# Four last chunks as two wide blocks, softmax steps ordered by a modelled clock, w_out sums on POOL

## The chip, the cores and the metric

The kernel runs on one core of a Trainium2 chip. The metric is the device time of one execution in microseconds (us). Engines are named as in the profile: PE is TensorE (matmuls, PEld its weight loads), DVE is VectorE, ACT is ScalarE, POOL is GpSimd, SP is SyncE, whose queue issues the DMAs.

## The reference, cut to what matters

Sliding-window attention of 8 batches x 8 heads over 576 positions of 64, then an MLP with elu on the 4608 tokens.

```python
scores = scale * np.matmul(q, k.transpose(0, 1, 3, 2))      # (8, 8, 576, 576), scale 1/8
mask_plain = (rel >= 0) & (rel < 32)                        # heads 0-3
mask_dil = (rel >= 0) & (rel < 128) & (rel % 4 == 0)        # heads 4-7
scores = np.where(masks, scores, -1e9)
attn = np.exp(scores - np.max(scores, -1)); attn = attn / (np.sum(attn, -1) + 1e-09)
x = (attn @ v).transpose(0, 2, 1, 3).reshape(4608, 512)
h = x @ w_in                                                # 512 x 2048
g = np.where(h > 0, h, np.exp(np.minimum(h, 0)) - 1)        # elu
out = g @ w_out                                             # 2048 x 512
```

## The kernel before

Every float32 operand of the MLP is split into a high part and a low rest, and a product is three products of parts. The 4608 tokens are nine chunks of 512. Chunks 0 to 2 multiply plainly. From chunk 3 (`CS`) on, the products are of the Strassen kind: seven products of half-sized operands take the place of eight, and sums and differences of blocks are made beside them on ACT and DVE.

- **Combined chunks** (3 to 6, `combined_chunk`): only h = x w_in is done with seven products. There are four groups `g` of seven steps, `ORDER` = A11 S2 S3 A12 S1 A22 S4; a step is 12 matmuls of 128x256 in `product`. A11, S2, S3 and A22 add up in one PSUM bank (`x_ps`), A12 in another (`y_ps`), which S1 opens anew and S4 adds to. Between them ACT copies the bank out: u1 after A11, u2 after S2, u3 after S3 (`TODO`, tile `e`), and DVE adds these to the other bank (C11 after A12, C22 after S1, C12 after S4). S2 and S3 write the bank that u1 and u2 read, so each waits for the copy. The second product of a group (elu(h) by w_out, 192 matmuls of 128x512 a chunk) waits in `fifo`; `pop(n)` after each step issues n parts of 3 matmuls, by `POPS`.
- **Wide block** (chunks 7 and 8 together, `wide_chunks`): both products are done with seven for eight, over 1024 tokens: 28 inner and 28 outer steps of 12 matmuls of 128x512. It needs sums of w_out blocks, made by `combine_out` on DVE and ACT (8 sets, each 4 sums of 128x256 and 2 rests of 128x512) in chunk 6 and in the block.
- **Attention** of batches 4 to 7 runs in the combined chunks. Heads go in pairs (four a batch). `PIECES` puts two pairs at a time between steps: a scores piece (144 matmuls, `scores_piece`) or an outputs piece (48 matmuls, `outputs_piece`). The softmax steps between them (`later_probabilities`: max, minus, exp on ACT, sum, reciprocal, times, then six small transposes a pair, all else on DVE) are put into the program by `work(SPARE[g][s])`, a budget for each step from a table.

Instructions of one engine keep program order (`inorder`). Helpers record many operations under one line: L124 is every matmul, L573 every ordered DVE and ACT instruction, L849 the load of stored w_in and w_out blocks (`load_combined`, four steps ahead by `RING`), L401 and L404 the copies of attention outputs.

Of the kernel before, what the change touches and what calls it, by code (L numbers as in the profile page):

```python
# [33 lines left out]
LASTC = NCH - 2  # L34
# [25 lines left out]
EARLY = 0.0  # L60
# [5 lines left out]
PIECES = {9: ("S", 2, 1), 14: ("O", 0, 1), 21: ("O", 2, 1), 23: ("S", 0, 2)}  # L66
# [20 lines left out]
def body(ctx: ExitStack, tc: tile.TileContext, q, k, v, masks, w_in, w_out, out, out_t):  # L87
# [35 lines left out]
    def mm(*args, **kw):  # L123
        return inorder(nc.tensor.matmul(*args, **kw))  # L124
# [204 lines left out]
    def combine_out(j):  # L329
# [3 lines left out]
        vec.tensor_tensor(out=a22, in0=a21, in1=a22, op=ALU.add)  # L333
        vec.tensor_tensor(out=a21, in0=a11, in1=a21, op=ALU.subtract)
        vec.tensor_tensor(out=a11, in0=a22, in1=a11, op=ALU.subtract)
        vec.tensor_tensor(out=a12, in0=a12, in1=a11, op=ALU.subtract)
        parts = []
        for w, names in zip(ws, (("S2", "S3"), ("S4", "S1"))):
            h, l = ap.tile([P, DM], F32R, name="vt"), w.bitcast(F32R)
            act.copy(out=h, in_=w)  # L340
            vec.tensor_tensor(out=l, in0=w, in1=h.bitcast(F32), op=ALU.subtract)
            parts += [(0, names, h), (1, names, l)]
        return parts
# [52 lines left out]
    def copies(b, hp, places, keep=lambda ins: ins):  # L396

        for a_ps, n0, n1 in places:
            flat, q0, q1 = a_ps[:, :(n1 - n0) * QB], n0 * QB, n1 * QB
            if hp >= NPAIR // 2:  # L400
                last = keep(nc.scalar.copy(out=x32[b][:, hp, q0:q1], in_=flat))  # L401
            else:
                dst = x32[b][:, hp, :].rearrange("p (c u) -> p c u", c=DIL)[:, :, q0 // DIL:q1 // DIL]
                last = keep(nc.scalar.copy(out=dst.rearrange("p c (s i) -> p s c i", i=G // DIL),  # L404
                                           in_=flat.rearrange("p (s c i) -> p s c i", c=DIL, i=G // DIL)))
        return last

# [159 lines left out]
    class Ordered:  # L567

        def __init__(self, eng):
            self.eng = eng  # L570

        def __getattr__(self, name):
            return lambda *args, **kw: inorder(getattr(self.eng, name)(*args, **kw))  # L573

    vec, act = Ordered(nc.vector), Ordered(nc.scalar)
    side, held = [], []

    def work(spare):

        while side and spare > 0:  # L580
            cost, step = side.pop(0)
            step()
            spare -= cost

    def later_probabilities(b, hps, groups):

        other_sm = slots("a5", 2, 3).rearrange("p o t -> p (o t)")[:QB, :2 * NU * 2 * G].rearrange("p (u j) -> p u j", u=2 * NU)
        sms = [ap.tile([QB, 2 * NU, 2 * G], F32, name="sm", bufs=1), other_sm]
        for j in (1, 0):
            masks_added(hps[j], groups[j], sms[j], vec)  # L590
        small = [[ap.tile([QB, 2 * NU], F32, name=n, bufs=4) for n in ("nmx", "sums")] for _ in hps]
        trs = [transposed() for _ in hps]
# [902 lines left out]
```

## Time and profile before

| | |
|---|---|
| median of 3 runs | 854.08 us (853.76 to 854.14) |
| profiled execution | 853.85 us, of which the profile's span is 852.0 us (1.85 us lie outside it) |
| mean granted TensorE clock | 0.997 of 2.4 GHz |
| PE busy | 839.9 us, 99% of the span |
| DVE, ACT, POOL busy | 657.6 us (77%), 486.5 us (57%), 8.7 us (1%) |
| chunk 3 begins at about | 317.5 us of the span |
| wide block | about 699.5 to 848.3 us |

Busy time is how long an engine had an instruction in it. The chain is followed back from the last instruction to what released it, so its shares say what the end of the kernel waited for.

### The profile page before, as it was taken

The page shows a single profiled execution, that of the slowest core. Times are in us where ns is not written, and L with a number is a line of the kernel's source. Part 1 is how long each engine was busy: PE and PEld are TensorE (multiplying, and loading weights), DVE is VectorE, ACT ScalarE, POOL GpSimd, SP SyncE. Part 2 cuts the span into 40 slices and gives each one's busy share as a digit, 9 for nine tenths or more (in the row PEclk, how much of TensorE's full clock was granted, in tenths as well). Part 3 has the DMA queues.
Part 4 walks back from the last instruction along what each step waited for, and adds up shares of the span by engine and source line. Part 5 has one row for each costly group of instructions (what it writes and reads, how often), then busy time and mean ns, then how long its engine had stood idle before and what let it go on. Part 6 is the DMA issues. An engine that isn't in the chain of part 4 may idle for free.

```text
span 852.0 us, 17515 instructions
## 1 busy us (share of the span) xinstructions
PE 839.9 (99%) x7080; PEld 704.0 (83%) x7080; DVE 657.6 (77%) x993; ACT 486.5 (57%) x835; POOL 8.7 (1%) x29
## 2 busy tenths in 40 slices
PE   6999999999999999999999999999999999999998
PEld 4566888888888889898999899899989988888886
DVE  5999998778588978965877587757877765786992
ACT  5889776645655465434644464544544556786460
POOL 3000000000000000000000000000000000000000
PEclk9999999999999999999999999999999999999999
DMA  8997457533677878757586667767675667997675
GB/s 301 378 378 304 138 170 237 163 112 107 204 253 237 266 206 258 242 181 244 179 262 195 193 219 221 251 186 218 193 237 189 212 209 240 334 353 247 188 222 170
DMA packets 99728, 193.73 MB, mean 227 GB/s; under 512 B 8800, under 2 KB 52160, under 8 KB 99648
## 3 DMA queue, kind: packets, MB, share of 16 engines
q1 hardware_dynamic: 99504, 192.30, 69.5%
q8 instruction: 56, 0.92, 0.4%
q10 hardware_dynamic: 144, 0.31, 0.1%
q14 instruction: 24, 0.20, 0.1%
HBM read 145.39 MB, written 47.19 MB: 226 GB/s over the span
## 4 chain that ended last, share of the span: by engine, by line
PE 97%; DMA 1%; ACT 1%; DVE 1%; issue 0%; SPq 0%; DVEq 0%; POOL 0%; ACTq 0%
PE o_ps L124 44%; PE h L124 41%; PE a_ps L124 11%; DMA r<-w_in 1%; DMA qt<-q 0%; ACT pt L490 0%; DVE nmx L450 0%; PE a L124 0%; DVE pt L488 0%; PE b L124 0%; PE d L124 0%; DVE sums L469 0%; ACT r L467 0%; DVE gh L573 0%; ACT x L404 0%
## 5 line engine op out<-in xcount | busy, mean ns | idle before, releaser
L124 PE MATMUL h<-xh,r 128*128 128x256 f32 (+1 forms) x728 | 171.7, 315 | 0.0
L124 PEld LDWEIGHTS h<-xh,r 128*128 128x128 f32 x728 | 123.6, 190 | 10.5 <-issue 0.2
L124 PE MATMUL o_ps<-a,r 128*128 128x512 f32 x528 | 127.0, 391 | 0.0
L124 PEld LDWEIGHTS o_ps<-a,r 128*128 128x128 f32 x528 | 97.3, 188 | 19.2
L124 PE MATMUL h<-xl,r 128*128 128x256 f32 (+1 forms) x364 | 109.0, 315 | 0.0
L124 PE MATMUL h<-a,r 128*128 128x256 f32 (+1 forms) x492 | 77.7, 308 | 0.0
L124 PE MATMUL o_ps<-a,gh 128*128 128x512 f32 x216 | 75.0, 444 | 0.0
L124 PEld LDWEIGHTS h<-a,r 128*128 128x128 f32 x492 | 69.6, 190 | 6.6
L124 PEld LDWEIGHTS h<-xl,r 128*128 128x128 f32 x364 | 69.3, 190 | 5.7 <-issue 0.2
L573 DVE SCALAR_TENSOR_TENSOR a-1_3460<-a-1_3460,a 128x1024 f32<-128x1024 f32 x32 | 39.1, 1222 | 37.3 <-ACT a L573 37.2
L573 ACT COPY e<-h 128x512 f32<-128x512 f32 x48 | 28.2, 588 | 56.3 <-PE h L124 55.5
L124 PE MATMUL o_ps<-r,r 128*128 128x512 f32 x220 | 57.5, 390 | 0.0
L124 PEld LDWEIGHTS o_ps<-a,gh 128*128 128x128 f32 x216 | 40.2, 188 | 17.3 <-issue 10.5
L573 DVE TENSOR_TENSOR a-1_3460<-h,e 128x512 f32<-128x512 f32 x48 | 33.0, 688 | 26.1 <-PE h L124 25.4
L124 PEld LDWEIGHTS o_ps<-r,r 128*128 128x128 f32 x220 | 40.6, 188 | 8.0
L573 ACT COPY a-1_3460<-h 128x512 f32<-128x512 f32 x16 | 9.4, 586 | 56.2 <-PE h L124 56.2
L124 PE MATMUL h<-r,r 128*128 128x256 f32 (+1 forms) x252 | 40.6, 311 | 0.0
L573 ACT ACTIVATE a<-a 128x1024 f32<-128x1024 f32 (+1 forms) x40 | 40.0, 1017 | 0.9
L716 ACT COPY h<-h 128x512 f32<-128x512 f32 x30 | 17.5, 584 | 39.8 <-PE h L124 39.6
L124 PE MATMUL o_ps<-r,gh 128*128 128x512 f32 x128 | 40.1, 395 | 0.0
L736 DVE TENSOR_TENSOR gl<-e,gh 128x512 fp32r<-128x512 f32 x37 | 25.4, 687 | 17.6 <-ACT gh L735 17.2
L124 PE MATMUL o_ps<-a,a 128*128 128x512 f32 x156 | 38.9, 391 | 0.0
(266 smaller groups left out, 1711.1 us busy)
## 6 DMA issues: line engine op xcount, KB each, us to landing
r<-combined SPq DMA_DIRECT2D x140, 512.0 KB, 4.4
vt<-v SPq DMA_DIRECT2D x30, 384.0 KB, 4.5
kt<-k SPq DMA_DIRECT2D x29, 304.0 KB, 4.3
qt<-q SPq DMA_DIRECT2D x30, 288.0 KB, 3.7
r<-w_in SPq DMA_DIRECT2D x16, 512.0 KB, 7.0
r<-w_out SPq DMA_DIRECT2D x16, 512.0 KB, 8.0
r<-sums_out SPq DMA_DIRECT2D x16, 512.0 KB, 4.7
r<-plain_out SPq DMA_DIRECT2D x12, 512.0 KB, 4.7
```

The lines of the kernel that those rows point to most:

```text
L124: return inorder(nc.tensor.matmul(*args, **kw))
L573: return lambda *args, **kw: inorder(getattr(self.eng, name)(*args, **kw))
L716: copied.append(a.copy(out=h, in_=h_ps).ins)
L736: low.append(v.tensor_tensor(out=gl, in0=e, in1=gh.bitcast(F32), op=ALU.subtract).ins)
```

## The change

The last four chunks become two wide blocks of 1024 tokens each (chunks 5 and 6, 7 and 8; `wide_chunk(w)`), and only chunks 3 and 4 stay combined. Attention of batches 4 to 7 is done one pair at a time: `pieces()` is called before each step and issues one pair's outputs or scores when the modelled clock says that what they need is there. The softmax steps (`pair_steps`) and the w_out sums are lists in `side`; `work(until)` emits those which by the modelled clock can end by `until`, where `clock` holds a time for PE, DVE, ACT and POOL and each `Ordered` engine adds a fixed cost and a cost by size. The six transposes of a pair become six ACT copies of 32x12x32 and one DVE transpose of 128x1152. The w_out sums move from DVE to POOL (their two copies stay on ACT) and are spread over chunks 3 and 4 and the first block by `COMBINE_AT` and `WIDE_COMBINE` (F fetch, C compute, W write, for each of 8 sets). T1 to T4, operands of the second block, are made on POOL during the last outer steps of the first (`NEXT`). Outputs of batches 5 and 6 that have no room yet go to DRAM and are fetched back (`staged`, `event`).

By the program, the 128x256 matmuls of the combined chunks go from 1360 to 688 and the 128x512 matmuls from 2504 to 2792. After the start of chunk 3 the program has 8 outputs pieces of two pairs before and 16 of one pair now, and 5 scores pieces of two pairs and 4 of one pair before and 14 of one pair now.

```diff
-LASTC = NCH - 2
+LASTC = NCH - 4
+NW = (NCH - LASTC) // 2
...
+COMBINE_AT = {2: "F0", 4: "C0", 6: "W0", 8: "F1", 10: "C1", 12: "W1", 14: "F2", 16: "C2", 18: "W2", 36: "F3", 39: "C3", 40: "W3", 41: "F4", 44: "C4", 45: "W4", 46: "F5", 49: "C5", 50: "W5"}
+WIDE_COMBINE = {9: "F6", 13: "C6", 14: "W6", 15: "F7", 18: "C7", 19: "W7"}
...
+NEXT = {21: "cast:B11 rest:B11 make:T1", 22: "make:T2 cast:B21 rest:B21", 23: "cast:T2 rest:T2", 24: "cast:T1 rest:T1 make:T3", 25: "cast:T3 rest:T3 make:T4", 26: "cast:T4 rest:T4",
+        27: "cast:B22 rest:B22"}
...
+STEP = 1.28
...
+LATENCY = 0.25
...
+ENDING = 0.0
+OVERRUN = (1.5, 2.5, 1.5, 2.5, 2.5, 2.5, 1.0)
...
+        elif what[0] == "C":
+            combined_out[j] = combine_out(j, rooms)
+        else:
+            last, parts = combined_out.pop(j)
+            until(*last)
+            store_sums(j, parts)
...
+        for to, x, y, op in ((a22, a21, a22, ALU.add), (a21, a11, a21, ALU.subtract), (a11, a22, a11, ALU.subtract), (a12, a12, a11, ALU.subtract)):
+            step(pool, "tensor_tensor", out=to, in0=x, in1=y, op=op)
+        hs = [rooms[1][i].bitcast(F32R) if rooms else fp.tile([P, DM], F32R, name="gh", bufs=3) for i in range(2)]
+        for w, h in zip(ws, hs):
+            step(act, "copy", out=h, in_=w)
+        for w, h, names in zip(ws, hs, (("S2", "S3"), ("S4", "S1"))):
+            l = w.bitcast(F32R)
+            step(pool, "tensor_tensor", out=l, in0=w, in1=h.bitcast(F32), op=ALU.subtract)
             parts += [(0, names, h), (1, names, l)]
-        return parts
+        side.append(steps)
+        return steps[-1][0], parts
...
+        def cost(self, kw):
+            return self.fixed + self.each * max(length(kw[n]) for n in ("out", "in_", "in0") if n in kw)
...
+            def emit(**kw):
+                clock[self.name] = self.free() + self.cost(kw)
+                return inorder(getattr(self.eng, name)(**kw))
+            return emit
+
+    vec, act, pool = Ordered(nc.vector, "DVE", 0.155, 0.00104), Ordered(nc.scalar, "ACT", 0.19, 0.00083), Ordered(nc.gpsimd, "POOL", 0.05, 0.0019)
...
+        name, eng, op, kw = pair.pop(0)
+        clock[eng.name] = max(eng.free(), finished.get(id(pair), 0.0))
+        getattr(eng, op)(**kw)
+        finished[id(pair)] = clock[eng.name] + LATENCY
...
+        while True:
+            side[:] = [pair for pair in side if pair]
+            starts = []
+            for n, pair in enumerate(side):
+                if ready_for(pair[0][0]):
+                    _, eng, _, kw = pair[0]
+                    start = max(eng.free(), finished.get(id(pair), 0.0))
+                    if start + eng.cost(kw) <= until:
+                        starts.append((start, pair[0][0][0] == "sums", n))
+            if not starts:
+                return
+            emit_next(side[min(starts)[-1]])
...
+    def pair_steps(b, hp, sm):
+
+        mx, sums = [ap.tile([QB, 2 * NU], F32, name=n, bufs=4) for n in ("nmx", "sums")]
+        tr = pt[hp % 2]
+        flat = tr.rearrange("p u q -> p (u q)")
         wide = lambda x: x.unsqueeze(2).broadcast_to([QB, 2 * NU, 2 * G])
-
-        def steps(j):
-
-            sm, (mx, sums), tr = sms[j], small[j], trs[j]
-            yield 0.9, lambda: vec.tensor_reduce(out=mx, in_=sm, op=ALU.max, axis=mybir.AxisListType.X)
-            yield 0.9, lambda: vec.tensor_tensor(out=sm, in0=sm, in1=wide(mx), op=ALU.subtract)
-            yield 0.0, lambda: act.activation(out=sm, in_=sm, func=AF.Exp, scale=0.125)
-            yield 0.9, lambda: vec.tensor_reduce(out=sums, in_=sm, op=ALU.add, axis=mybir.AxisListType.X)
-            yield 0.1, lambda: vec.tensor_scalar(out=sums, in0=sums, scalar1=1e-9, scalar2=None, op0=ALU.add)
-            yield 0.1, lambda: vec.reciprocal(out=sums, in_=sums)
-            yield 0.9, lambda: vec.tensor_tensor(out=sm, in0=sm, in1=wide(sums), op=ALU.mult)
-            for c in range(GU):
-                for r in range(2):
-                    ks, cs, rs = slice((c + r) * G, (c + r + 1) * G), slice(c * G, (c + 1) * G), slice(r * G, (r + 1) * G)
-                    yield 0.57, lambda ks=ks, cs=cs, rs=rs: vec.transpose(out=tr[ks, :, cs], in_=sm[cs, :, rs])
-
-        one, other = list(steps(0)), list(steps(1))
-        side.extend([*one[:2], other[0], one[2], other[1], one[3], other[2], *one[4:7], *other[3:7]])
-        (held if hps[0] else side).extend(one[7:] + other[7:])
-        return [(b, hp, tr) for hp, tr in zip(hps, trs)]
+        yield ("max", b, hp), vec, "tensor_reduce", dict(out=mx, in_=sm, op=ALU.max, axis=mybir.AxisListType.X)
+        yield ("less", b, hp), vec, "tensor_tensor", dict(out=sm, in0=sm, in1=wide(mx), op=ALU.subtract)
+        yield ("exp", b, hp), act, "activation", dict(out=sm, in_=sm, func=AF.Exp, scale=0.125)
+        yield ("sum", b, hp), vec, "tensor_reduce", dict(out=sums, in_=sm, op=ALU.add, axis=mybir.AxisListType.X)
+        yield ("more", b, hp), vec, "tensor_scalar", dict(out=sums, in0=sums, scalar1=1e-9, scalar2=None, op0=ALU.add)
+        yield ("over", b, hp), vec, "reciprocal", dict(out=sums, in_=sums)
+        yield ("times", b, hp), vec, "tensor_tensor", dict(out=sm, in0=sm, in1=wide(sums), op=ALU.mult)
+        for c in range(GU):
+            for r in range(2):
+                yield ("placed", b, hp, c, r), act, "copy", dict(out=tr[(c + r) * G:(c + r + 1) * G, :, c * G:(c + 1) * G], in_=sm[c * G:(c + 1) * G, :, r * G:(r + 1) * G])
+        yield ("turned", b, hp), vec, "transpose", dict(out=flat, in_=flat)
...
+        if outputs_too and to_output and to_output[0][0] < output_limit and output_ready():
+            one_output(*to_output[0])
+        elif scores_ready():
+            one_scores(*to_score[0])
...
+                t = (c - CS) * NG * 7 + step
+                for what in PLAN.get(t, "").split():
+                    event(what)
+                pieces(t >= OUTPUTS_FROM, B - 1)
+                for what in COMBINE_AT.get(t, "").split():
+                    combining(what)
+                tick()
...
+                clock["now"] = clock["PE"]
...
-                    elif what[0] == "w":
-                        work(SPARE[g][s])
...
-                pop((FIRST_POPS[g] if c == CS and g < 2 or c == NCH - 3 and g == 1 else POPS)[s])
...
+                pop((FIRST_POPS[g] if c == CS and g < 2 else POPS)[s])
+                work(clock["PE"] + STEP + OVERRUN[s])
...
+                (vec, pool)[w].tensor_tensor(out=t[:, :, r0:r1], in0=x0, in1=x1, op=ALU.subtract)
...
-    work(EARLY)
+    clock["now"] = clock["PE"]
+    clock["DVE"] = clock["ACT"] = clock["PE"] + ENDING
+    work(clock["PE"] + STEP + OVERRUN[-1])
...
-    wide_chunks()
+    for w in range(NW):
+        wide_chunk(w)```

**Order of the instructions.** First ACT's row as chunk 3 begins: `COPY e<-h` are u1, u2 and u3 of the first group, `CAST xh` and `CAST x_` splits of operands, the ACTIVATEs on 96x768 the exps of two pairs whose scores were taken in chunk 2. Before:

```order
L573 CAST r_1360<-e 128x512
L573 COPY e<-h_3671 128x512
L573 CAST xh_3450<-x_1958 128x2x192
L573 CAST xh_3450<-x_3026 128x2x64
L573 COPY e<-h_3671 128x512
L573 CAST xh_3452<-a_2290 128x512
L573 COPY e<-h_3671 128x512
L573 ACTIVATE sm<-sm 96x768
```

And of the change:

```order
L627 CAST r_1358<-e 128x512
L627 COPY e<-h_3657 128x512
L627 CAST x_3440<-x_1952 128x2x192
L627 CAST x_3440<-x_3016 128x2x64
L627 ACTIVATE sm<-sm 96x768
L627 ACTIVATE a_2284<-a_2284 96x768
L627 COPY e<-h_3657 128x512
L627 CAST x_3441<-a_2284 128x512
L627 COPY e<-h_3657 128x512
```

Both exps now stand ahead of u2; they stood behind u3.

DVE at the same place: the TENSOR_REDUCEs to 96x12 are the max (`nmx`) of each pair, the TENSOR_TENSORs on 96x768 its subtraction. Before:

```order
L573 TENSOR_TENSOR a_1632<-e,r_1360 128x512
L573 TENSOR_REDUCE nmx<-sm 96x12
L573 TENSOR_TENSOR xl_3451<-x_1958,xh_3450 128x2x192
L573 TENSOR_TENSOR xl_3451<-x_3026,xh_3450 128x2x64
L573 TENSOR_TENSOR sm<-sm,nmx 96x768
L573 TENSOR_TENSOR a_2290<-x_1958,a_2290 128x2x192
L573 TENSOR_TENSOR a_2290<-x_3026,a_2290 128x2x64
L573 TENSOR_REDUCE nmx<-a_2290 96x12
L573 TENSOR_TENSOR a_2290<-a_2290,nmx 96x768
```

And of the change:

```order
L627 TENSOR_TENSOR a_1626<-e,r_1358 128x512
L627 TENSOR_REDUCE nmx<-sm 96x12
L627 TENSOR_REDUCE nmx<-a_2284 96x12
L627 TENSOR_TENSOR x_3440<-x_1952,x_3440 128x2x192
L627 TENSOR_TENSOR x_3440<-x_3016,x_3440 128x2x64
L627 TENSOR_TENSOR sm<-sm,nmx 96x768
L627 TENSOR_TENSOR a_2284<-a_2284,nmx 96x768
L627 TENSOR_TENSOR a_2284<-x_1952,a_2284 128x2x192
L627 TENSOR_TENSOR a_2284<-x_3016,a_2284 128x2x64
```

The two pairs' maxima and subtractions now stand together, ahead of the operand difference a<-x,a.

PE around an outputs piece in the combined chunks (`pt` the probabilities, `vt` the values). Before, two pairs:

```order
L124 MATMUL h_4042<-xh_3456,r_936 128x256 x2
L124 MATMUL a_ps_4131<-pt_80,vt 64x96 x10
L124 MATMUL a_ps_4132<-pt_80,vt 64x96 x2
L124 MATMUL a_ps_4132<-pt_79,vt 64x96 x8
L124 MATMUL h_4133<-pt_79,vt 64x96 x4
L124 MATMUL h_4168<-a_1748,r_936 128x256 x12
```

And of the change, one pair:

```order
L147 MATMUL h_3871<-r_1358,r_934 128x256 x12
L147 MATMUL o_ps<-a_1742,r_1176 128x512 x9
L147 MATMUL a_ps_4025<-pt_80,vt 64x96 x6
L147 MATMUL a_ps_4026<-pt_80,vt 64x96 x6
L147 MATMUL h_4046<-x_3440,r_934 128x256 x12
L147 MATMUL o_ps<-a_1742,r_1176 128x512 x3
```

PE leaves the wide products twice as often for pieces half as long.

## Rows read from the trace of the kernel before

**Rows 1.** The page: its head, PE's busy time (share of the span, instructions), and the shares of the chain that ended last, by engine.

```profile
span 852.0 us, 17515 instructions
PE 839.9 (99%) x7080; PEld 704.0 (83%) x7080; DVE 657.6 (77%) x993; ACT 486.5 (57%) x835; POOL 8.7 (1%) x29
...
PE 97%; DMA 1%; ACT 1%; DVE 1%; issue 0%; SPq 0%; DVEq 0%; POOL 0%; ACTq 0%
```

**Rows 2.** Windows of two periods of a combined chunk (from one outputs piece to that of the next chunk) and of the wide block: stretch, its length, then busy time and instructions of PE, PEld, DVE, ACT and POOL, the granted clock, the DMA engines' busy share and GB/s.

```profile
450.70:543.10 92.40, 92.40 (x914) 83.30 (x913) 67.29 (x105) 45.26 (x64) 0.19 (x2) 1.00 0.68 215
543.10:635.96 92.86, 92.86 (x914) 83.34 (x913) 66.64 (x105) 45.25 (x64) 0.19 (x2) 1.00 0.68 212
...
699.50:852.00 152.50, 148.75 (x657) 122.78 (x655) 109.38 (x131) 87.73 (x112) 0.00 (x0) 1.00 0.75 248
```

**Rows 3.** The chain in order of time: start, length, engine, output, line, instructions. The first two lie in a combined chunk (o_ps are second products of 128x512, h two steps of 128x256), the other two in the wide block (all 128x512).

```profile
396.62 2.75 PE o_ps L124 x12
399.37 2.87 PE h L124 x24
...
704.07 2.72 PE o_ps L124 x12
...
837.37 10.89 PE h L124 x48
```

**Rows 4.** The timeline of PE around pieces (start, length, operation): one pair's scores in a combined chunk, two pairs' scores, one pair's outputs in chunk 0, two pairs' outputs. Each piece is given by its first row (scores have many) and the row behind it.

```profile
342.92 0.24 PE L124 MATMUL h<-kt,qt 64*32 64x64 f32 x1
...
343.82 0.96 PE L124 MATMUL o_ps<-a,r 128*128 128x512 f32 x3
...
391.87 0.24 PE L124 MATMUL h<-kt,qt 64*32 64x64 f32 x1
...
393.49 0.98 PE L124 MATMUL h<-r,r 128*128 128x256 f32 x6
...
65.02 1.21 PE L124 MATMUL a_ps<-pt,vt 128*64 128x96 f32 x24
66.16 2.41 PE L124 MATMUL o_ps<-a,gh 128*128 128x512 f32 x5
...
450.91 1.87 PE L124 MATMUL a_ps<-pt,vt 128*64 128x96 f32 x40
...
453.05 1.22 PE L124 MATMUL h<-a,r 128*128 128x256 f32 x8
```

**Rows 5.** The timeline as chunk 3 begins, DVE, then ACT, then PE; in brackets the idle time before an instruction and what ended it. On PE, h<-a,r is S2 and h<-r,r is S3.

```profile
319.65 0.69 DVE L573 TENSOR_TENSOR a<-e,r 128x512 fp32r<-128x512 f32 x1 [0.69 <-ACT r L573]
320.26 0.94 DVE L573 TENSOR_REDUCE nmx<-sm 96x12 f32<-96x768 f32 x1
321.12 0.74 DVE L573 TENSOR_TENSOR xl<-x,xh 128x384 fp32r<-128x384 f32 x2
321.79 0.95 DVE L573 TENSOR_TENSOR sm<-sm,nmx 96x768 f32<-96x768 f32 x1
322.66 0.75 DVE L573 TENSOR_TENSOR a<-x,a 128x384 f32<-128x384 f32 x2
...
319.53 0.58 ACT L573 COPY e<-h 128x512 f32<-128x512 f32 x1
320.00 0.71 ACT L573 CAST xh<-x 128x384 fp32r<-128x384 f32 x2
321.94 0.59 ACT L573 COPY e<-h 128x512 f32<-128x512 f32 x1 [1.22 <-PE h L124]
...
325.24 0.84 ACT L573 ACTIVATE sm<-sm 96x768 f32<-96x768 f32 x1
...
320.31 1.59 PE L124 MATMUL h<-a,r 128*128 128x256 f32 x12
321.74 0.63 PE L124 MATMUL o_ps<-r,gh 128*128 128x512 f32 x2
...
323.13 1.59 PE L124 MATMUL h<-r,r 128*128 128x256 f32 x12
```

**Rows 6.** Groups of instructions by line and shape from 451 to 543 us: busy time, mean ns of one, idle time before them.

```profile
L573 DVE STREAM_TRANSPOSE pt<-a 32x384 f32<-32x384 f32 x12 | 6.8, 568 | 0.2
...
L573 DVE TENSOR_TENSOR sm<-a_ps,masks_sb 96x384 f32<-96x384 f32 x4 | 2.0, 544 | 0.0
...
L573 DVE TENSOR_REDUCE sums<-sm 96x12 f32<-96x768 f32 x2 | 1.9, 940 | 0.0
...
L401 ACT COPY x<-a_ps 128x384 f32<-128x384 f32 x1 | 0.5, 511 | 0.0
```

**Rows 7.** The same view from 636 to 852 us, of DVE: two of the w_out sums.

```profile
L573 DVE TENSOR_TENSOR qt<-qt,vt 128x512 fp32r<-128x512 f32 x8 | 5.5, 693 | 6.9 <-ACT vt L573 6.9
...
L573 DVE TENSOR_TENSOR qt<-kt,qt 128x256 f32<-128x256 f32 x8 | 3.4, 425 | 0.3
```

**Rows 8.** The timeline of POOL and of DVE near the start of the kernel, where POOL has an operation with two inputs. (`d` is a PSUM tile.)

```profile
17.35 1.47 POOL L415 TENSOR_TENSOR r<-r,sums 96x768 f32<-96x768 f32 x1 [0.74 <-ACT pt L490]
...
18.05 0.95 DVE L465 TENSOR_TENSOR r<-d,nmx 96x768 f32<-96x768 f32 x1
```

**Rows 9.** DMA issues of the stored blocks (count, KB each, median us to landing), and what SP's queue waited for at their line (us in total, times, longest).

```profile
r<-combined SPq DMA_DIRECT2D x140, 512.0 KB, 4.4
...
SPq L849 <- PE h L124: 241.3, 112, 5.7
```

More of the change, by code (lines that the diff above doesn't have):

```diff
@@ new lines, in body, with one_scores @@
+    to_score, to_output = [[(b, hp) for b in range(CS + 1, B) for hp in range(NPAIR)] for _ in range(2)]
+    del to_score[:2]
+    landed = {}
+    banks_free = [0.0]
+    def one_scores(b, hp):
+        to_score.pop(0)
+        s_ps = banks()
+        i = b * NPAIR + hp
+        scores(s_ps, *qk_of.pop(i), True)
+        clock["now"] = clock["PE"]
+        sm = sms[hp % 2]
+        masks_added(hp, [[(0, NU, a)] for a in s_ps], sm, vec)
+        banks_free[0] = clock["DVE"] + LATENCY
+        side.append(list(pair_steps(b, hp, sm)))
+        finished[id(side[-1])] = clock["DVE"]
+        load_qk(i + 2)
+        landed["qk", i + 2] = clock["PE"] + LANDING
@@ new lines, in one_output @@
+    def one_output(b, hp):
+        to_output.pop(0)
+        places = [(a, i * NA, (i + 1) * NA) for i, a in enumerate(banks())]
+        i = b * NPAIR + hp
+        products(places, v_of.pop(i), pt[hp % 2])
+        clock["now"] = clock["PE"]
+        if b not in outputs_of and b not in x32:
+            x32[b] = xp.tile([P, NPAIR, S], F32, name="x32", bufs=2)
+        copies(b, hp, places, act)
+        banks_free[0] = clock["ACT"] + LATENCY
+        taken_out.add((b, hp))
+        load_v(i + 2)
+        landed["v", i + 2] = clock["PE"] + LANDING
@@ L1179, in wide_chunks @@
             i = base + k
+            if w == 0:
+                for what in WIDE_COMBINE.get(k, "").split():
+                    if what[0] == "F":
+                        wide_rooms = [[fp.tile([P, DM], F32, name=n, bufs=m) for _ in range(2)] for n, m in (("gl", 2), ("gh", 3))]
+                    combining(what, wide_rooms)
+                for what in WIDE_PLAN.get(k, "").split():
+                    event(what)
+                if k in PIECES_AT:
+                    if k == PIECES_AT[0]:
+                        kept.append(sms[1])
+                        sms[1] = space(1).rearrange("p o t -> p (o t)")[:QB, :2 * NU * 2 * G].rearrange("p (u j) -> p u j", u=2 * NU)
+                    pieces()
+                if k == KEPT_UNTIL:
+                    assert all(kw.get("in_") is not kept[0] for pair in side for *_, kw in pair)
             load_combined(i + RING)
+            tick()
             if kind == "in":
-                if name == "A11":
-                    banks_of[g] = banks_for(g)
+                if name in ("A11", "A12"):
+                    banks_of[g, name == "A12"] = two(("ah", "oo", "ho", "oh")[g][name == "A12"])
                 tos = inner(i, g, name)
-                if g == 0 and k < 5:
+                clock["now"] = clock["PE"]
+                if w == g == 0 and k < 5:
                     for what in TODO[k]:
@@ L1219, in wide_chunks @@
                 outer_done[0] += 1
-                tick()
+                clock["now"] = clock["PE"]
                 make_units(2)
+                if w < NW - 1:
+                    for what in NEXT.get(outer_done[0] - 1, "").split():
+                        wide_operand(w + 1, what)
                 if n == NG:
@@ L1233, in wide_chunks @@
                         added(us["o", 2], over_banks["Q"], ("o", 2))
+                    elif name == "S4" and w < NW - 1:
+                        drawn(stored("C12", tos, ("o", 2)))
+            if w == 0:
+                work(clock["PE"] + (WIDE_STEP if kind == "in" else OUTER_STEP))
     def second_attention():
@@ L1422, in body @@
                 take_places()
-                moving["temporary"], late = [halved(slots("a5", o)) for o in range(2)], moving["temporary"]
                 for what in sum(OPERANDS[:7], []):
```

319 lines of the change are left out of this document (177 added, 142 removed).

## The prediction

> **What bounds the kernel now.** I read the page first: PE is busy for 99% of the span and 97% of the chain that ended last is PE [rows 1]. No other engine's busy share decides anything while that holds, so I price the change in PE time and then ask where PE would have to wait. Next the windows by stage: PE is busy for the whole of a combined chunk's period, 92.40 and 92.86 us, with DVE at 73% and ACT at 49% of it, POOL nearly idle [rows 2]. Then the chain for the pace of PE in each kind of stage: in a combined chunk 12 matmuls of 128x512 take 2.75 us and 24 of 128x256 take 2.87; in a wide block 12 of 128x512 take 2.72, and 48 take 10.88 to 10.89 [rows 3]. Last the timeline, for attention pieces and the start of chunk 3 [rows 4, 5].
>
> **Products.** A combined chunk has 336 matmuls of 128x256 and 192 of 128x512: 14 x 2.87 + 16 x 2.75 = 84.2 us [rows 3]. The windows check this. Two scores pieces of two pairs take 391.87 to 393.49 = 1.62 us each, two outputs pieces of two pairs 450.91 to 453.05 = 2.14 each [rows 4]; 84.2 + 2 x 1.62 + 2 x 2.14 = 91.7 of 92.40 [rows 2], which leaves 0.7 for four visits, 0.18 each. The second period has one scores piece of two pairs, two of one pair (342.92 to 343.82 = 0.90) and the same outputs: 84.2 + 1.62 + 1.80 + 4.28 = 91.9 of 92.86, 0.19 for each of five visits. So entering and leaving a piece costs about 0.2 us, and there is no other wait in these periods. Two combined chunks go: 168.4 us. One wide block comes, 56 steps of 12: 56 x 2.72 = 152.3 us. Products: **-16.1 us**.
>
> By counts it is the same thing: 672 matmuls of 120 ns less, 288 of 227 to 229 more, about -15 us with the chunks' switches left out. The Trainium skill ("TensorE: Matmul & The Clock Gate", section "Wait — 56ns, not 53.3ns?") gives N columns at 2.4 GHz plus about 2.5 ns; an estimate from it is 109 and 216 ns, and -11.2 us in place of -16.1. The rows disagree with it here by 10% and 5% (119.6 and 226.7 ns), and I take the rows.
>
> **Pieces.** Before, after the start of chunk 3: 8 x 2.14 + 5 x 1.62 + 4 x 0.90 = 28.8 us, and 17 visits x 0.2 = 3.4: 32.2. Now 16 outputs of one pair, 65.02 to 66.16 = 1.14 each [rows 4], and 14 scores of 0.90: 30.8, and 30 visits x 0.2 = 6.0: 36.8. Pieces: **+4.6 us**.
>
> **The start of chunk 3.** The clock's start (`ENDING` 0) takes DVE and ACT as free when chunk 3 begins. They are not: chunk 3 begins at about 317.5, and DVE still does the elu rest of chunk 2 at 319.65 [rows 5]. So the emitted order puts max, max, minus, minus and both exps early, and u2 behind both exps (the order of ACT above). S3 writes the bank that u2 reads. Before, u2 went at 321.94 as soon as S2 was through, and S3 began at 323.13 after two pops, never waiting. With the new order and these durations (starts apart by the spacing of the rows): max sm 320.26, max a 321.12, the two xl 321.98, minus sm 322.65, minus a 323.52 to 324.47; exp sm 323.6 to 324.45; exp a 324.5 to 325.35 (0.84); u2 325.3 to 325.9 (0.59); S3 at about 325.95 instead of 323.13. PE stands **2.8 us**, which nothing gives back: it is in order. Late next would be C11, on DVE behind the same steps, but PE's own stall has let DVE catch up, so I price that at nothing. The bounds are nothing, if the engines get there sooner than so, and 4 us, if DVE's later rows (0.75 for a<-x,a [rows 5]) get in front too.
>
> **DVE and ACT.** A pair loses six transposes of 0.568 = 3.4 us of DVE and gains one of 128x1152, which no row shows: 0.57 if it costs as a 32x384, 1.70 if by its elements (1152/384 x 0.568). It gains six ACT copies, 0.51 each by a copy of 128x384 [rows 6]: 3.1 us. I take 1.4 for the transpose, nearer to the upper end since the element count is the row's own axis; for 16 pairs DVE loses 32 us (27 to 45) and ACT gains 49. With six pairs a chunk instead of four, DVE needs about 71 and ACT about 70 of a period of about 95 us (from 67.3 and 45.3 [rows 2], a pair at about 6.5 and 5.1). Neither is the bound. Cost **0**; without that cover it would be what the copies wait, below.
>
> **w_out sums.** They take 4 x 0.425 + 2 x 0.69 = 3.1 us a set from DVE [rows 7], eight sets, 25 us, hidden under PE. On POOL 768 elements take 1.47 us [rows 8], so 256 about 0.49 and 512 about 0.98: 3.9 us a set, 31 for all, and T1 to T4 of block two 1.96 each, 8 more. What waits for them is SP's writes (W), and behind these in SP's queue the loads of stored blocks. A load lands in 4.4 us, and it is issued when PE frees its place [rows 9], four steps of about 3.0 us (84.2/28) ahead, three of which count: 9.0 - 4.4 leaves 4.6 us, more than a whole set's 3.9. Cost **0**; the bounds are 0 and 8 sets x 3.9 = 31 us if each set's end were waited for in full.
>
> **Sum.** 853.85 - 16.1 + 4.6 + 2.8 = 845.15 us on the profiled execution; the median of before is 0.23 above that execution, so **845.4 us**. The wide block's own banks, and its change from one block to the next, I price at nothing by the block of before, whose 152.50 us are 152.3 of steps [rows 2].
>
> **Rivals.**
> - *A, the sum as it stands*: 845.4, its own range 843.8 to 848.5. Chance 0.50.
> - *D, no stall at chunk 3*: the exps come early enough, or u2 isn't what S3 waits for; for it, DVE's rows of before hold small gaps; against it, the order of ACT. 842.6. Chance 0.13.
> - *B, more copies queue behind softmax steps*: C11 must be through before S1, 4 pops or 4 x 0.69 = 2.76 us after A12 (a pop is half of the 1.39 from 321.74 to 323.13 [rows 5]). A score's two mask adds (1.09), two steps of 0.95 and C11 itself (0.69) make 3.7 us: 0.9 too much. If that or its like happens at a third of the 14 scores pieces, it is 4.4 us: 849.8. For it, the modelled clock's times are as far off at other places as at chunk 3; against it, DVE is a quarter idle. Chance 0.20.
> - *C, the other side: POOL's sums hold DVE up.* About 16 bursts of 1.96 us (two a set), during which DVE's operations with two SBUF inputs stand still. If PE loses 0.8 us by each, 12.8 us and 858.2; it ends slower than before from (855.8 - 845.4)/16 = 0.65 us a burst on. For it: such operations are most of DVE's work here, and no row of before shows one beside POOL. Against: a DVE operation with one SBUF and one PSUM input took its 0.95 us beside POOL [rows 8], and at chunk 3 of before u2 was through at 322.53 and S3 came at 323.13, 0.6 us of cover where only two pops stand between [rows 5], and elsewhere there are more. Chance 0.09. The Trainium skill ("SBUF — State Buffer", section "SBUF: two separate sides") has it that DVE with two SBUF inputs and POOL exclude each other for a whole instruction; no run here shows it yet, and by that rule this rival is the one to fear.
> - *E, SP's queue*: writes wait for POOL longer than 4.6 us, loads come late at, say, 8 sets by 1.5 us: 857.4. Chance 0.03.
> - *F, matmuls at N columns plus a fixed 2.5 ns*, by the page of the first part: 850.3. In rows: it would need 227 ns for 512 columns to become 216 in the new stages. Chance 0.02.
>
> The rest, 0.03, I leave to a mishap of above 858.
>
> **How the numbers follow.** The time is A's: 845.4. The range holds D, A and B and their bounds (B twice as bad: 854.2): 842.0 to 854.0, about 0.83. A difference under 0.2%, 1.7 us, can't be told from none; "same" is 852.4 to 855.8. Faster: D 0.13, A 0.50, F 0.02, and 0.17 of B's 0.20 = 0.82. Same: 0.03 of B, 0.03 of C, 0.02 of E = 0.08. Slower: the remaining 0.10.
>
> **What would show it.** In the profile of the change: two combined chunks of 84.2 us of products and two blocks of 152.3; pieces of 1.14 and 0.90 with 0.2 around each; one PE wait of 2.8 us near 323 to 326, ended by ACT's copy of the bank; a transpose of 128x1152 between 0.57 and 1.70 us; POOL operations near 0.49 and 0.98 with DVE's 0.69 and 1.22 unchanged beside them. Wrong would be: no wait there (D), waits of PE for DVE or ACT all along chunks 3 and 4 (B), DVE or POOL operations longer than those of before where both run (C), loads landing after PE wants them (E).

## The result and the profile after

The changed kernel takes 861.69 us (median of 4 executions, 858.80 to 861.86) against 854.11 before: 1.0081 times as long, 95% interval 1.0060 to 1.0103. The forecast was 845.4, with a range of 842.0 to 854.0. The profiled execution is the shortest of the four, 858.80 us (span 856.9); the other three took 861.58 to 861.86.

The page of the change answers to [rows 1]; its columns are the same.

```profile
span 856.9 us, 16854 instructions
PE 832.8 (97%) x6696; PEld 679.1 (79%) x6696; DVE 640.9 (75%) x871; ACT 546.6 (64%) x935; POOL 75.2 (9%) x78
...
PE 89%; DMA 3%; ACT 3%; DVE 2%; issue 1%; POOL 1%; SPq 0%; DVEq 0%; ACTq 0%; POOLq 0%
```

PE works 7.1 us less than before, yet the span is 4.9 longer: the chain is no longer PE from end to end. The windows show where (stretch, length, PE busy, PEld, DVE, ACT, POOL, granted clock, DMA, GB/s; [rows 2] are those of before).

```profile
317.50:412.00 94.50, 88.68 (x1017) 76.88 (x1016) 68.39 (x94) 64.06 (x105) 19.77 (x18) 0.98 0.83 268
412.00:512.00 100.00, 99.30 (x1125) 86.84 (x1124) 74.00 (x99) 71.95 (x115) 21.21 (x18) 1.00 0.91 300
512.00:536.00 24.00, 24.00 (x124) 20.57 (x123) 18.55 (x26) 17.62 (x26) 0.00 (x0) 1.00 0.52 169
536.00:690.00 154.00, 148.98 (x856) 121.83 (x855) 111.20 (x115) 97.89 (x132) 20.21 (x16) 0.99 0.67 210
690.00:845.00 155.00, 155.00 (x686) 128.38 (x685) 100.67 (x104) 87.34 (x105) 6.01 (x4) 1.00 0.68 207
```

PE stands 5.8 us in the first stretch and 5.0 in the first wide block, 0.7 in chunk 4 and nothing in the second block. Three waits make nearly all of it; everywhere else from 317.5 to 845 PE stands less than 1 us in all. The timeline of PE at each (start, length, operation, idle time before it and what ended it; a wait is named below by the start of the last matmul ahead of it, and its length is counted from matmul to matmul, beyond the usual pace):

```profile
322.79 0.39 PE L147 MATMUL o_ps<-r,gl 128*128 128x512 f32 x1
325.76 0.50 PE L147 MATMUL h<-r,r 128*128 128x256 f32 x2 [2.58 <-ACT e L627]
...
346.78 2.91 PE L147 MATMUL o_ps<-a,r 128*128 128x512 f32 x12
352.71 0.50 PE L147 MATMUL h<-r,r 128*128 128x256 f32 x2 [3.02 <-ACT e L627]
...
603.83 2.19 PE L147 MATMUL a_ps<-pt,vt 128*64 128x96 f32 x24 [5.01 <-DVE pt L627]
```

**At 322.8** S3 waits for u2: the wait that was forecast, 2.75 us.

**At 349.3** S3 of the next group waits for its u2 too, 3.2 us. ACT's timeline there tells why:

```profile
347.06 0.51 ACT L627 COPY pt<-a 32x384 f32<-32x384 f32 x1
352.08 0.58 ACT L627 COPY e<-h 128x512 f32<-128x512 f32 x1 [4.50 <-DMA out<-e]
```

u2 needs one of four buffers `e`; the output stores of chunk 2 use the same four, and ACT, busy with softmax copies and the copies of the w_out sums, made those outputs late. The chain has `345.64 6.34 DMA out<-e` ahead of the copy. In the kernel before, u2 waits for a store at this place too, 0.8 us, but PE does not wait there (ACT of before):

```profile
342.45 0.59 ACT L573 COPY e<-h 128x512 f32<-128x512 f32 x1 [0.77 <-DMA out<-e]
```

**At 598.4** an outputs piece waits 5.2 us for its transpose. The chain ahead of it (start, length), then POOL, DVE and ACT there:

```profile
581.28 4.61 DMA sums_out<-gl
...
586.81 5.73 DMA gl<-whole_out
...
592.66 4.01 POOL L627 TENSOR_TENSOR gl<-gl 128x256 f32<-128x256 f32 x4 [10.14 <-DMA gl<-whole_out]
596.75 2.53 POOL L627 TENSOR_TENSOR gl<-gl,gh 128x512 fp32r<-128x512 f32 x2
599.24 2.08 POOL L627 TENSOR_TENSOR x<-x,x 128x896 f32<-128x896 f32 x1
...
599.27 3.13 DVE L627 TENSOR_TENSOR r<-a,r 128x1024 fp32r<-128x1024 f32 x1 [5.64 <-ACT r L627]
602.32 1.36 DVE L627 STREAM_TRANSPOSE pt<-pt 128x1152 f32<-128x1152 f32 x1
...
595.88 0.62 ACT L627 CAST gh<-gl 128x512 fp32r<-128x512 f32 x1 [2.98 <-POOL gl L627]
```

Two things stack. ACT's two copies of the last set of w_out sums wait in program order for POOL, POOL for the fetch of the blocks, and everything of ACT behind them is late, among it the cast that DVE's r<-a,r needs. The fetch was late in its turn: it goes into the two buffers `gl`, and the set before had to be stored out of them first (the first two rows). Then that DVE operation takes 3.13 us instead of 1.22: it starts beside POOL's first operation for T1, which ends at 601.32, and ends 1.1 us behind that, at 602.40, as if it had begun only then. The transpose stands behind it. T1 was not meant to run here: its place in the program is among the last outer steps of the block, which ends at about 690, but nothing that POOL waits for holds it back, so POOL starts it right behind the sums.

Two of the waits cost more than themselves. PE's granted clock is 0.66 from 325.8 to 330 after it stood 2.6 us, and 0.69 from 603.8 to 609 after 5 us, so part of each at the lower level of 1.2 GHz. Behind the wait at 349.3, of 3.0 us, it stayed at 1.00 (the last row):

```profile
325.80:330.00 4.20, 4.20 (x22) 3.91 (x23) 3.86 (x8) 2.75 (x6) 3.61 (x4) 0.66 0.38 103
603.80:609.00 5.20, 5.17 (x35) 4.46 (x36) 2.88 (x4) 1.76 (x3) 0.00 (x0) 0.69 0.27 108
...
352.70:356.00 3.30, 3.29 (x20) 2.99 (x21) 1.19 (x1) 3.25 (x5) 2.95 (x4) 1.00 1.07 403
```

4.2 x 0.34 + 5.2 x 0.31 = 3.0 us are lost by that in this execution.

### The profile page after: what moved, and what is told of

Its sections match the earlier page's. It is cut to its first block, busy times and chain, and to the rows that moved or that the text cites. A ratio compares the mean times of both kernels' runs of the same rounds, so it can differ in the third digit from the quotient of the medians.

```text
span 856.9 us, 16854 instructions
## 1 busy us (share of the span) xinstructions
PE 832.8 (97%) x6696; PEld 679.1 (79%) x6696; DVE 640.9 (75%) x871; ACT 546.6 (64%) x935; POOL 75.2 (9%) x78
## 4 chain that ended last, share of the span: by engine, by line
PE 89%; DMA 3%; ACT 3%; DVE 2%; issue 1%; POOL 1%; SPq 0%; DVEq 0%; ACTq 0%; POOLq 0%
PE o_ps L147 44%; PE h L147 33%; PE a_ps L147 11%; DMA r<-combined 1%; DMA out<-e 1%; DMA gl<-whole_out 1%; ACT a L627 1%; PE b L147 1%; POOL gl L627 1%; DMA sums_out<-gl 1%; DMA qt<-q 0%; PE a L147 0%; ACT pt L627 0%; ACT pt L536 0%; ACT e L627 0%
## 5 line engine op out<-in xcount | busy, mean ns | idle before, releaser
L147 PE MATMUL o_ps<-a,r 128*128 128x512 f32 x672 | 159.8, 390 | 0.0
L147 PEld LDWEIGHTS o_ps<-a,r 128*128 128x128 f32 x672 | 125.1, 188 | 25.8
L147 PE MATMUL h<-x,r 128*128 128x256 f32 (+1 forms) x708 | 131.8, 337 | 0.2 <-DMA r<-combined 0.2
L147 PEld LDWEIGHTS h<-x,r 128*128 128x128 f32 x708 | 109.6, 191 | 16.2 <-PE h L147 0.4
L147 PE MATMUL o_ps<-r,r 128*128 128x512 f32 x384 | 93.7, 390 | 0.0
L147 PE MATMUL h<-a,r 128*128 128x512 f32 (+1 forms) x456 | 89.3, 347 | 0.0
L147 PEld LDWEIGHTS h<-a,r 128*128 128x128 f32 x456 | 74.1, 190 | 11.6 <-issue 0.2
L147 PEld LDWEIGHTS o_ps<-r,r 128*128 128x128 f32 x384 | 71.6, 188 | 14.8 <-DVE r L627 0.3
L147 PE MATMUL o_ps<-a,gh 128*128 128x512 f32 x216 | 75.0, 444 | 0.0
L147 PEld LDWEIGHTS o_ps<-a,gh 128*128 128x128 f32 x216 | 40.2, 188 | 17.3 <-issue 10.5
L147 PE MATMUL o_ps<-r,gh 128*128 128x512 f32 x128 | 40.5, 398 | 0.0
L147 PE MATMUL a_ps<-a,r 128*128 128x512 f32 x168 | 39.4, 389 | 0.0
L147 PEld LDWEIGHTS a_ps<-pt,vt 128*64 128x64 f32 x640 | 28.2, 140 | 13.5 <-ACT x L627 6.1
L147 PE MATMUL a_ps<-pt,vt 128*64 128x96 f32 x640 | 32.9, 254 | 5.2 <-DVE pt L627 5.0
L147 PE MATMUL h<-r,r 128*128 128x256 f32 (+1 forms) x168 | 30.9, 333 | 6.2 <-ACT e L627 6.2
L147 PEld LDWEIGHTS a_ps<-a,r 128*128 128x128 f32 x168 | 31.5, 188 | 6.5
L627 ACT ACTIVATE x<-x 128x1024 f32<-128x1024 f32 (+1 forms) x33 | 34.8, 1056 | 0.5
L627 ACT COPY pt<-sm 32x384 f32<-32x384 f32 x48 | 24.5, 511 | 16.2 <-DVE sm L627 15.5
L147 PE MATMUL h<-x,a 128*128 128x512 f32 (+1 forms) x128 | 34.3, 416 | 0.0
L147 PEld LDWEIGHTS h<-r,r 128*128 128x128 f32 x168 | 25.7, 190 | 10.8 <-ACT e L627 7.4
## 6 DMA issues: line engine op xcount, KB each, us to landing
r<-combined SPq DMA_DIRECT2D x112, 512.0 KB, 4.8
r<-sums_out SPq DMA_DIRECT2D x32, 512.0 KB, 4.7
r<-plain_out SPq DMA_DIRECT2D x24, 512.0 KB, 4.3
r<-w_in SPq DMA_DIRECT2D x16, 512.0 KB, 7.0
r<-w_out SPq DMA_DIRECT2D x16, 512.0 KB, 8.1
```

What stands on the lines that cost most here:

```text
L147: return inorder(nc.tensor.matmul(to, w, x, **kw))
L627: return inorder(getattr(self.eng, name)(**kw))
```

## The experiments

Three theories: (1) single waits at single places; (2) POOL's use of SBUF holds DVE up all along chunks 3 and 4, the forecast's rival C; (3), which came with the second run, that at the start of chunk 3 too much work of DVE and ACT is due, so that a wait there can be moved but not taken away.

### The change again

> The changed kernel unchanged, as the control of the runs beside it. Its first profile (858.8 us) has three large waits of PE: 2.7 us at 322.8 (S3 behind ACT's copy u2), 3.2 us at 349.3 (the copy u2 of the next group, which waits for a store of the output to leave its buffer), and 5.2 us at 598.4 (an outputs piece behind a transpose of DVE). Its other three executions took 861.6 to 861.9. If these waits hang on when DMAs land, the profile here shows the same three places with one of them longer by about 3 us; if they hang on compute alone, all three keep their length and the 3 us are somewhere else.

860.92 us (858.48 to 863.76), 1.0079 times before (1.0053 to 1.0104). This is the control of the runs that follow. Its profile (858.48) has the same waits: 2.75 us at 322.7, 2.82 at 347.7, 4.52 at 597.8. But the clock does not follow them as it did in the first profile. It stayed at 1.00 behind the first wait and fell behind the second (columns as above):

```profile
325.80:330.00 4.20, 4.20 (x30) 3.98 (x31) 4.17 (x9) 2.90 (x6) 3.01 (x3) 1.00 0.47 140
350.70:356.00 5.30, 5.24 (x21) 4.27 (x21) 3.12 (x4) 3.38 (x6) 2.94 (x4) 0.68 0.88 313
```

The four executions lie 5.3 us apart, so a difference of medians of a few runs can be off by a us or two, and where a profile gives the length of a wait, that is the better measure of it.

### The copy u2 ahead of the exps

```diff
-        getattr(eng, op)(**kw)                      # in emit_next
+        if behind_u2 is not None and (behind_u2 or name[0] == "exp"):
+            clock[eng.name] = eng.free() + eng.cost(kw)
+            behind_u2.append(lambda: inorder(getattr(eng.eng, op)(**kw)))   # handed out right after u2
+        else: getattr(eng, op)(**kw)
```

(The code is shortened.)

> Only the two exps at the start of chunk 3 are emitted behind the copy u2; every other instruction keeps its place. Theory 1 (single waits at single places): the 2.7 us wait of PE at 322.8 and the lower clock behind it (0.66 for 4.2 us, 1.4 us) go, so 4 us less than the control, unless the wait at 349.3 grows by what PE is now earlier (then 0 to 2 us less). Theory 2 (POOL's sums hold up DVE all along chunks 3 and 4): the wait goes here but DVE's held operations come back as other waits, less than 1 us gained.

862.64 us (858.36 to 864.08): no gain, against theory 1. S3 no longer waits; S1 does, 2.9 us. PE, DVE and POOL of this run:

```profile
328.22 0.39 PE L147 MATMUL o_ps<-r,r 128*128 128x512 f32 x1
331.35 1.67 PE L147 MATMUL h<-x,r 128*128 128x256 f32 x12 [2.74 <-ACT x L627]
...
328.20 1.31 DVE L627 TENSOR_TENSOR sm<-sm,sums 96x768 f32<-96x768 f32 x1
329.44 1.21 DVE L627 TENSOR_TENSOR x<-a,x 128x512 fp32r<-128x512 f32 x1
330.57 0.68 DVE L627 TENSOR_TENSOR a-1_3444<-h,e 128x512 f32<-128x512 f32 x1
...
327.14 4.09 POOL L627 TENSOR_TENSOR h<-h 128x256 f32<-128x256 f32 x4 [14.18 <-DMA h<-whole_out]
```

The last DVE row is C11. It ends at 331.25, and S1, which opens its bank anew, starts at 331.35; the ACT cast that the row of PE names was done by then. DVE had seven softmax operations ahead of C11. That is theory 3. Theory 2 has a share: the two operations just ahead of C11 took 1.31 and 1.21 us beside POOL's sums, where the same forms take 0.95 and 0.68 elsewhere, so 0.9 of the 2.9 us is that.

### The last w_out set later

```diff
-WIDE_COMBINE = {9: "F6", 13: "C6", 14: "W6", 15: "F7", 18: "C7", 19: "W7"}
+WIDE_COMBINE = {9: "F6", 13: "C6", 14: "W6", 15: "F7", 22: "C7", 23: "W7"}
```

> The last set of w_out sums (C7, its ACT copies and its stores) is placed four steps later in the first wide block; nothing else moves. Theory 1: at 598 ACT stood 3.0 us behind the copy of that set, which waited for POOL, which waited for a fetch; and DVE was held 1.9 us by POOL's T1. With the set later, ACT and DVE reach the transpose before the outputs piece, PE's 5.2 us and about 1.6 us of lower clock go: 5 to 7 us less than the control. Theory 2: sums are as many and as long as before, and the time stays within 1.5 us of the control.

856.28 us (853.08 to 859.39), 4.6 less than the control, a little under the 5 to 7 expected. The wait at 598 is gone. The hold of DVE by T2 now reaches PE; in the change it was there too (3.14 us at 638.97), but PE was late and did not notice. DVE, POOL and PE:

```profile
639.54 3.13 DVE L627 TENSOR_TENSOR a<-a 128x1024 f32<-128x1024 f32 x1
642.60 1.47 DVE L627 TENSOR_TENSOR r<-a,r 128x1024 fp32r<-128x1024 f32 x1
...
638.89 4.10 POOL L627 TENSOR_TENSOR x<-x,x 128x896 f32<-128x896 f32 x2 [22.06 <-ACT x L627]
...
644.12 1.20 PE L147 MATMUL o_ps<-r,r 128*128 128x512 f32 x4 [1.44 <-DVE r L627]
```

This profile (859.39) also has 2.5 us at 523, as the wide block begins. The chain there is `519.48 5.94 DMA r<-combined`, a load issued late: SP's queue had stood 3.8 us for the read-back of attention outputs (`SPq L768 <- DMA outputs<-gl: 3.8, 1, 3.8`), with the loads of stored blocks behind it.

### The last store of chunk 2 in another buffer

```diff
-        o = fp.tile([P, DM], F32, name="e") if c < CS else ...
+        o = fp.tile([P, DM], F32, name="e") if c < CS and (c, t) != (CS - 1, 3) else ...   # then gl
```

> The last of the four output stores of chunk 2 uses a buffer of gl instead of one of the four buffers e that the copies u1 to u3 use. If the wait at 349.3 is that of u2 for the store's buffer, it goes: about 3.2 us less than the control. If it is ACT being late by its own queue, the wait stays and the time is the control's.

856.20 us (854.97 to 857.83), 4.7 less than the control by the medians, 3.5 by the two profiled executions; 3.2 was expected. Its profile has no wait at 345 to 350; those at 322.6 (2.75) and 594.8 (4.09) stay, and a load of stored blocks comes 1.5 us late near 375. So the wait at 349.3 is that for the buffer.

### Both, and then T1 to T4 on DVE

The first run has the two edits above, the second this one as well:

```diff
-                (vec, pool)[w].tensor_tensor(out=t[:, :, r0:r1], in0=x0, in1=x1, op=ALU.subtract)
+                vec.tensor_tensor(out=t[:, :, r0:r1], in0=x0, in1=x1, op=ALU.subtract)
```

> Two edits together: the last output store of chunk 2 in a buffer of gl, and the last w_out set four steps later. Each alone gave 4.6 to 4.7 us against the control run beside it. If the waits are single places that don't feed each other, the gains add: about 851.5 (860.9 - 9.4). If what one removes only makes another wait longer (as putting the copy u2 first did), 854 to 856.

851.95 us (849.69 to 855.43), 0.9972 of before (0.9959 to 0.9984): 9.0 less than the control, so the gains add.

> As e_and_c7, and T1 to T4 of the second block are made on DVE, not on POOL. The trace with C7 late shows a DVE operation of 128x1024 that took 3.05 us instead of 1.22 at 639.6, and PE waiting 1.6 us right behind. If POOL's operation held it, the hold and that wait go: 1 to 2 us less than e_and_c7. If DVE was late by itself, putting four more operations on DVE makes no gain or costs up to 4.9 us.

848.75 us (848.20 to 849.43), 0.9934 of before (0.9919 to 0.9949), 3.2 less than without the third edit and more than the 1.6 us of the one wait; where the rest comes from is not shown. DVE's operations of 128x1024 there take 1.22 us again. Its profile has a single large wait left:

```profile
326.74 1.50 PE L147 MATMUL h<-r,r 128*128 128x256 f32 x8 [2.58 <-ACT e L627]
```

> The same kernel as e_c7_t1dve, beside held_and_later and timed more often: 848.7 within 1 us, with one large wait of 2.7 us near 323.

849.07 us (848.90 to 851.03), 0.9933 (0.9920 to 0.9945). This version is faster than the kernel before and than the change.

### The w_out sums on DVE, and left out

```diff
-            step(pool, "tensor_tensor", out=to, ...)        # and the two rests
+            step(on_vec, "tensor_tensor", out=to, ...)      # DVE, with POOL's modelled times
```

> The sums of w_out blocks at the same places of the program as in the change, but on DVE, not on POOL (T1 to T4 stay on POOL); all else as the change. Theory 2 (the shared use of SBUF with POOL is what the change lost): DVE's operations of 1024 elements all go back to 1.22 us in chunks 3 and 4 and the time falls by 5 us or more. Theory 1 (single waits): DVE works 25 us more in program order, and as it then stands itself behind the fetches from DRAM, the time stays within 2 us of the control's 860.9 or gets longer; the waits at 322.7 and 347.7 stay.

857.81 us (856.78 to 858.73), 1.0041 of before, 3.1 less than the control: between what the two theories said. The waits at 323 (2.74) and 349.5 (2.76) stay, that at 601.7 falls to 2.0. DVE's operations of 128x1024 are back at 1.21 to 1.22 us in all groups but two, those that meet T1 to T4, which were still on POOL:

```profile
L627 DVE TENSOR_TENSOR r<-a,r 128x1024 fp32r<-128x1024 f32 x4 | 5.1, 1283 | 1.1 <-ACT r L627 1.1
...
L627 DVE TENSOR_TENSOR a<-a 128x1024 f32<-128x1024 f32 x1 | 3.1, 3139 | 0.0
```

In the change the first of these groups had a mean of 1759. So the hold is real. What it costs by itself this run can't say: DVE also got POOL's work, and three new waits of PE of 0.4 to 0.7 us came up. It is far from the 12.8 us of rival C.

> The adds, subtracts and rests of the w_out blocks are left out (their fetches, their two copies on ACT and their stores stay), so that POOL has only T1 to T4 to do. Theory 2: 5 us or more less than the control, and none of DVE's operations in chunks 3 and 4 longer than alone. Theory 1: the waits at 322.7 (2.7 us) and 347.7 (2.8 us) stay, as they have nothing to do with the sums; of that at 598 (4.5 us and its lower clock) some 3 us go, for ACT's copies wait for the fetch alone: 2 to 4 us less than the control.

851.51 us (849.48 to 851.84), 9.4 less than the control by the medians and 6.9 by the profiled executions: as much as theory 2 asked for, but not at its places. The wait at 349 falls to 1.85 and that at 598 is gone altogether, more than theory 1 expected: without the sums, T1 no longer falls beside the transpose. Those two places give 5.5 us. Two smaller waits came up (1.4 and 0.5 us near 444), and the mean granted clock is 0.997 where the control's profile has 0.992, which is some 4 us. What speaks against theory 2 is the profile of the change: outside its three waits PE stands less than 1 us from 317.5 to 845.

> e_c7_t1dve with the w_out sums on DVE too, at the same places of the program, so that POOL does nothing. It asks what the move of the sums to POOL is worth by itself once the large waits are gone. If 25 us of DVE's work were hidden under PE anyway (as the forecast has it), the same time as e_c7_t1dve within 1.5 us. If POOL's use of SBUF costs PE something all along, faster by more than that; if DVE is short of time in chunks 3 and 4, slower by 2 us or more.

852.77 us (850.65 to 854.44): 4 us more than with the sums on POOL. Its profile has waits of 0.4 to 0.8 us at seven places beside the one near 323. Once nothing critical meets POOL, POOL is the better place.

### The backlog at chunk 3, moved twice more

```diff
+                    if (c, g) == (CS, 0):       # steps from the first exp on are kept, and handed out here
+                        release({"u2": 2, "C11": 1, "C22": 3, "C21": 100}.get(what, 0))
```

(The code is shortened; the second run's move of the outputs piece is not in it.)

> e_c7_t1dve, and at the start of chunk 3 the first two pairs' softmax steps from the exps on are handed out behind the copies they stood ahead of: both exps behind u2, one sum behind C11, the rest of the first pair behind C22, all else behind C21. Putting u2 first alone only moved the wait to S1 (2.9 us at 328.2, behind C11 on DVE). If DVE's backlog of softmax steps is what both waits come from, the 2.7 us at 323.8 and the lower clock behind it (1.4 us) go and nothing comes in their place: 844.5 to 846, which is the forecast's sum without its 2.8 us and with the 1 to 2 us of small waits that stay. If the pair's transpose now comes after its outputs piece (336.8), 1 to 2 us come back: 846 to 848.

850.10 us (849.09 to 852.97): no gain on 848.75, against every number expected. S3 and S1 go through, and the first outputs piece waits:

```profile
335.30 0.39 PE L147 MATMUL o_ps<-r,a 128*128 128x512 f32 x1
338.46 1.21 PE L147 MATMUL a_ps<-pt,vt 128*64 128x96 f32 x24 [2.77 <-DVE pt L627]
```

> held_behind, and the first outputs piece of chunk 3 one step later (all other pieces where they were). With the steps held back, the wait of 2.7 us went from S3 to that piece (2.9 us at 335.3), which needs the last copies and the transpose of the first pair. If the same backlog is behind all three places, giving the piece a step of about 2.8 us more takes the wait away: 845 to 847, and no wait over 0.5 us between 318 and 345. If the piece then holds up the scores that follow it in the same banks, or the late copies hold up u1 of the next group, 1 to 3 us stay.

851.32 us (849.89 to 852.89), 2.2 more than its neighbour on the same chip (849.07). The outputs piece no longer waits; inside the pieces that follow, PE stands 3.7 us at 339.6, ahead of the scores, which need the banks that ACT's copies of the outputs free. Four places, 2.75, 2.9, 2.9 and 3.7 us: theory 3 fits all four. It is not shown, since no run took work out of the stretch or gave it more time, and part of a later wait is of the new order's making: in held_behind two ACT copies of the second pair, 1.0 us, stand among the six that the outputs piece of the first pair needs.

The trace of before says which of the two it is more likely to be. There the same two pairs go through with PE busy all the time from 317.5 to 356, though DVE does twelve transposes of 0.57 us for them. But its first outputs piece comes 19 us later (before, then the change):

```profile
358.50 1.87 PE L124 MATMUL a_ps<-pt,vt 128*64 128x96 f32 x40
...
339.51 1.21 PE L147 MATMUL a_ps<-pt,vt 128*64 128x96 f32 x24
```

So the early piece, more than the amount of work, seems to make the stretch tight. To start attention's pieces later throughout, or to give PE other work there (more pops), was not tried.

## Why the prediction was wrong

**Right: products and pieces.** Each piece of the change takes 1.14 or 0.90 us and 0.19 to 0.24 around it, as [rows 4] had it, and chunk 4 and the second block have one wait between them, of 0.7 us. PE's busy time fell by 7.1 us, or 10.1 with the 3.0 us of lower clock left out, where the two terms (16.1 less, 4.6 more) make 11.5. The version without the other waits (848.2 to 849.4 against 845.4, with 1.7 us of lower clock behind the first wait and a small wait of 0.7) bears the sum out to about 2 us.

**Right: the stall at chunk 3.** Forecast 2.8 us with S3 at 325.95; measured 2.75 with S3 at 325.76. Its price left out the clock behind it, 1.4 us here and nothing in the second profile of the same kernel. That C11 would not be late next held for the reason given: PE's own wait gave DVE the time, and in u2_first, where S3 did not wait, C11 was late.

**Right: the transpose.** 1.37 us, taken as 1.4 of 0.57 to 1.70.

**Wrong: "w_out sums ... Cost 0".** This is the step that failed. It asked only what SP's queue holds behind the writes. It did not ask what stands behind the two copies that each set leaves on ACT: they wait for POOL, which waits for a fetch, and ACT's later casts wait with them. And outside rival C it listed T1 to T4 at 1.96 us of POOL without asking what DVE does beside them. Together that is the wait at 598: 5.2 us and 1.6 us of clock. c7_late takes the wait away by moving the set and, behind it, T1; in e_c7_t1dve DVE's operations are back at 1.22 us. How the 5.2 us divide is read from the trace alone: the hold is 1.9 of them. POOL's prices were low too: a sum of 128x256 took 0.73 us at the least and 0.95 in the mean, a rest 1.29 at the least, not 0.49 and 0.98, so [rows 8] did not scale.

**Wrong: "DVE and ACT ... Cost 0".** The load of both is about what was forecast: 68 us of DVE and 64 of ACT in a stretch of 94.5, 74 and 72 in one of 100, against 71 and 70 of 95. The mean hid that ACT's added copies come in bursts and hand a buffer back late: 3.2 us at 349.3, shown by e_to_gl. None of the rows that the forecast went by points at the buffers `e`. The trace of before does, with its 0.77 us of ACT behind `DMA out<-e`, and so does the code, since `store` and u1 to u3 draw from one ring of four.

**Rival C** had the right mechanism and the wrong size. Beside POOL, DVE's operation with two SBUF inputs took 3.13 us instead of 1.22 and ended 1.1 us after POOL's. The Trainium skill ("SBUF — State Buffer", section "SBUF: two separate sides") has it that the two exclude each other for a whole instruction; the trace agrees. But the holds that are seen to reach PE are few: ahead of the transpose at 598, of an operand's rest at 644 in c7_late, and of C11 in u2_first.

From 845.15 to the 858.80 of the profile: 3.2 at 349.3, 5.2 at 598.4, 3.0 of clock, 1.1 in two waits of 0.4 and 0.7 us; 1.2 is not accounted for. The median of the change lies another 2.9 above that execution.

**Open:** the executions of the change lie up to 5.3 us apart, those of before within 2.4. Two things on record go with the longer ones. One is the granted clock: 0.994 in the execution of 858.80 us, 0.990 to 0.992 in those of 861.58 to 861.86, and 0.002 to 0.004 of 860 us is 1.7 to 3.4. The other is late loads of stored blocks: the profile of u2_first, of 863.47 us, has 1.2 us for one near 379 and 2.1 at 521, that of the change only 0.4 at 380. The wait at 520 to 523 comes behind the read-back of outputs and is in two other profiles (2.5 us in c7_late, 1.3 in held_and_later). No run changed either.

## What to carry to other kernels

When work moves to an idle engine, follow each thing that it hands back: who copies it, on which engine in program order, and what stands behind that copy. A mean load of three quarters hides nothing by itself; ask where a burst meets a buffer ring or a bank that PE needs next. When removing a wait moves it to the next place with the same length, look for what makes the whole stretch tight, in work or in a consumer that comes too early, before trying another order.

## What the runs showed of the hardware

A DVE operation on 128x1024 with both inputs in SBUF took 3.13 us beside POOL operations on SBUF, 1.22 alone. POOL took 0.73 us for 128x256 where 1.47 for 96x768 [rows 8] had suggested 0.49. The clock behind a wait is not the same each time: PE stood the same 2.6 us near 323 in ten profiles; behind it the granted clock fell to the level of 1.2 GHz for a few us in seven, the change among them (0.66 over 4.2 us, 1.4 us lost), and stayed at 2.4 in three (again, e_to_gl, e_c7_t1_sums_dve). It fell behind all five waits in which PE stood 3.5 to 5.0 us.
